# Ordering the first microseconds of a fused attention and GLU kernel: statistics on VectorE, the first tile's K ahead of the second tile's Q, Wk loaded earlier

## The chip, the cores and the metric

The kernel runs on one core of one Trainium2 chip. The metric is the device time of the whole program in microseconds (us), lower is better. Every ratio below is between runs of granted clock 0.999 or 1.0. Times inside a profile count from the start of its span, which is 1.7 to 1.9 us shorter than the measured time.

## The reference, cut to what matters

```python
xn = layernorm(x)                      # x: 1 x 2048 x 512, bf16
a = attention(xn, wqkv, wo)            # 32 heads of 16, a local window of 8 positions, dilation 2
b = (gelu(xn @ w_gate) * (xn @ w_up)) @ w_down
return x + a + b
```

Everything starts with the normalisation of x, and the attention branch starts with Q, K and V = xn @ wqkv. The kernel works on blocks of 512 rows. The first block is cut into four row tiles of 128 rows, so that TensorE can begin before all of it is normalised. For each tile: load x, statistics, subtract the mean, multiply by 1/std (sqrt on ScalarE, reciprocal on VectorE), transpose on TensorE, copy the transpose out of PSUM, project.

## The kernel before

The kernel is a graph of tasks. A list scheduler, when the program is built, orders each engine's tasks from a model of time; `chain([...])` forces an order. The parts that the change touches:

```python
# order of the first loads: a lower prio is issued earlier
x tiles 0, 1, 2, 3:   prio -960, -959, -957.8, -956.5
Wq, Wk, Wv:           prio -958, -957.5, -898

# the second tile (t == 1) has its statistics on ScalarE, in two passes with an accumulator
sx1   = activation(Identity, accum_out=sum)          # sum of x
negm1 = activation(Identity, scale=-1/512)           # minus the mean
sxx1  = activation(Square, bias=-mean, accum_out=..) # sum of squares
...
# warm-up matmuls of ones: WARM[0] ahead of the first transpose, WARM[1] behind it
WARM = ([512] * 9 + [128], [512, 128, 128, 128, 128])
...
# VectorE, ScalarE and TensorE of the first block
chain(["bnst0", "bnag0", "sub0", "rstd0", "norm0", "mean1", "sub1", "evy0_0", "rstd1", "norm1", "evy0_1", "bnst2", ...])
chain(["sx1", "sq0", "negm1", "sxx1", "sq1", "evx0_0", "evx0_1", "evq0_0", "sq2"])
chain(["evx1_0", "sq3"])
chain(WARM[0] + ["tpx0_0"] + WARM[1] +
      ["mma0_0", "tpx0_1", "mmt0_0", "mmt0_1", "mmt1_0", "tpx1_0", "mmt1_1", "mmt0_2", "tpx1_1", ...])
```

In these names `tpx0_0, tpx0_1, tpx1_0, tpx1_1` are the transposes of tiles 0 to 3, and `evx`/`evy` the copies of a transpose by ScalarE and VectorE. `mmt0_t` is Q of tile t (16 matmuls of 128 columns) and `mmt1_t` its K; `mma0_0` is the first half of tile 0's Q, whose other half is then `mmt0_0`. `evq0_t`, `evk0_t` are ScalarE's copies of Q and K out of PSUM, and `sq_t` is a tile's sqrt.

Of the kernel before, what the change touches and what calls it, by code (L numbers as in the profile page):

```python
# [622 lines left out]
BF = mybir.dt.bfloat16  # L623
F32 = mybir.dt.float32
# [47 lines left out]
def bass_parallel_sum__sliding_local_dilated__glu_gated_geglu__prompt_kernel(nc, A_x, A_wqkv, A_wo, B_x, B_w_gate, B_w_up, B_w_down, out, dbg=None, cfg=None):  # L672
# [40 lines left out]
    with contextlib.ExitStack() as es:  # L713
# [29 lines left out]
        sums = sb("sums", [128, 3], F32)  # L743
        XS = sb("XS", [128, 512], BF)
# [64 lines left out]
        I_sums = Item("sums")  # L809
        I_xs = Item("XS")  # L810
        I_junk = Item("junk")
# [54 lines left out]
        for i, wn in enumerate(WARM[0] + WARM[1]):  # L866
            it_warm = Item("warm%d" % i, P_ps, "warm")

            def mk_w(it=it_warm, wn=wn):
                return lambda e: e.matmul(PS[:, 512 * it.slot:512 * it.slot + wn], lhsT=one_l,  # L870
                                          rhs=one_r[:, 0:wn], start=True, stop=True)
            t_w = G.task("pe", "warm%d" % i, d_mm(wn), mk_w(), wr=[it_warm], prio=-400, mode="f")
            t_w.urgent = True
            warm_tasks.append(t_w)
# [43 lines left out]
        for p in range(NP):  # L918
# [5 lines left out]
            if p < 2:  # L924
                for t2 in range(2):
                    def mk_ld(t2=t2, p=p, it=it_x):
                        return lambda e: e.dma_start(  # L927
                            XIN[:, it.slot, t2, :], x2[256 * p + 128 * t2:256 * p + 128 * t2 + 128, :])
                    t_x = G.task("sp", "ld_x%d_%d" % (p, t2), 0, mk_ld(), wr=[(it_x, t2)],
                                 prio=((-960, -959), (-957.8, -956.5))[p][t2], nbytes=128 * 1024)  # L930
            else:
                def mk_ld(p=p, it=it_x):
                    return lambda e: e.dma_start(
                        XIN[:, it.slot, :, :], x2[256 * p:256 * p + 256, :].rearrange("(t q) d -> q t d", q=128))
                t_x = G.task("sp", "ld_x%d" % p, 0, mk_ld(), wr=[(it_x, 0), (it_x, 1)],
                             prio=(0, 0, -897.5, -897)[p] if p < 4 else -950 + p * 20, nbytes=256 * 1024)
# [3 lines left out]
            for t2 in range(2):  # L940
                t = 2 * p + t2

                def mk_st(t=t, t2=t2, it=it_x):
                    return lambda e: e.bn_stats(out=st[:, t, :], in_=XIN[:, it.slot, t2, :])  # L944
                if t == 1:
                    for (nm, dur, kw, rd, wr) in (
                            ("sx1", 0.55, dict(out=XR[:, 0, :], func=ACTF.Identity, accum_out=sums[:, 0:1]),
                             [], [I_junk, (I_sums, 0)]),
                            ("negm1", 0.2, dict(out=sums[:, 1:2], in_=sums[:, 0:1], func=ACTF.Identity,
                                                scale=-1.0 / D), [(I_sums, 0)], [(I_sums, 1)]),  # L950
                            ("sxx1", 0.55, dict(out=XR[:, 0, :], func=ACTF.Square, bias=sums[:, 1:2],
                                                accum_out=sums[:, 2:3]), [(I_sums, 1)], [I_junk, (I_sums, 2)])):
                        def mk_a(kw=kw, it=it_x):
                            return lambda e: e.activation(**dict(dict(in_=XIN[:, it.slot, 1, :]), **kw))
                        t_of[nm] = G.task("act", nm, dur, mk_a(), rd=rd + ([] if "in_" in kw else [(it_x, 1)]),
                                          wr=wr, prio=-300)
                    t_of["mean1"] = G.task("dve", "mean1", 0.1, lambda e: e.tensor_scalar(
                        out=mv[:, 1, 0:1], in0=sums[:, 0:1], scalar1=1.0 / D, scalar2=None, op0=ALU.mult),
                        rd=[(I_sums, 0)], wr=[(I_mv, 1)], prio=tp0(t))
                    continue  # L960
                t_of["bnst%d" % t] = G.task("dve", "bnst%d" % t, 0.6, mk_st(), rd=[(it_x, t2)], wr=[(I_st, t)], prio=tp0(t))

                def mk_ag(t=t):
                    return lambda e: e.bn_aggr(out=mv[:, t, :], in_=st[:, t, :])
                t_of["bnag%d" % t] = G.task("dve", "bnag%d" % t, 0.09, mk_ag(), rd=[(I_st, t)], wr=[(I_mv, t)], prio=tp0(t) + 1)
            for ts in (((2 * p,), (2 * p + 1,)) if b == 0 else ((2 * p, 2 * p + 1),)):
# [6 lines left out]
                def mk_sa(t=t):  # L973
                    if t == 1:
                        return lambda e: e.activation(out=sq[:, 1:2], in_=sums[:, 2:3], func=ACTF.Sqrt,
                                                      scale=1.0 / D, bias=eps[:, 0:1])
                    return lambda e: e.activation(out=sq[:, t:t + 1], in_=mv[:, t, 1:2], func=ACTF.Sqrt,
                                                  bias=eps[:, 0:1])
                if t < NSQA:
                    t_of["sq%d" % t] = G.task("act", "sq%d" % t, 0.15, mk_sa(), rd=[(I_sums, 2) if t == 1 else (I_mv, t), I_eps],  # L980
                                              wr=[(I_sq, t)], prio=pr - 100, table="sqrt")
                else:
                    t_of["ve%d" % t] = G.task("dve", "ve%d" % t, 0.09, mk_ve(), rd=[(I_mv, q) for q in ts],
                                              wr=[(I_ve, q) for q in ts], prio=pr + 1)
# [13 lines left out]
            for t2 in range(2):  # L998
# [6 lines left out]
                if t == 1:  # L1005
                    def mk_sub(it=it_x):
                        return lambda e: e.tensor_scalar(
                            out=XS[:, :], in0=XIN[:, it.slot, 1, :], scalar1=mv[:, 1, 0:1], scalar2=None,
                            op0=ALU.subtract)
                t_of["sub%d" % t] = G.task("dve", "sub%d" % t, 0.27, mk_sub(), rd=[(it_x, t2), (I_mv, t)],  # L1010
                                           wr=[I_xs if t == 1 else (it_x, t2)], prio=tp0(t) + 2)

                def mk_nm(t=t, t2=t2, it=it_x):
                    return lambda e: e.tensor_scalar(  # L1014
                        out=XIN[:, it.slot, t2, :], in0=XS[:, :] if t == 1 else XIN[:, it.slot, t2, :], scalar1=rstd[:, t:t + 1],
                        scalar2=None, op0=ALU.mult)
                t_of["norm%d" % t] = G.task("dve", "norm%d" % t, 0.27, mk_nm(), rd=[I_xs if t == 1 else (it_x, t2), (I_rstd, t)],
# [55 lines left out]
        chain(["bnst0", "bnag0", "sub0", "rstd0", "norm0", "mean1", "sub1", "evy0_0", "rstd1", "norm1",  # L1073
# [5 lines left out]
        for b in range(NB):  # L1079
# [7 lines left out]
            if b == 0:  # L1087
                lead = []
                for t in range(4):
                    for which in range(2):  # L1090
# [17 lines left out]
                        if t == 0 and which == 0:  # L1108
                            t_mm = G.task("pe", "mma0_0", 8 * 0.0563, mk_mm((0, 1)), rd=mrd, wr=[it_mm],
                                          prio=-100, mode="f")  # L1110
                            t_mm.urgent = True
                            t_of["mma0_0"] = t_mm
# [18 lines left out]
                chain(["sx1", "sq0", "negm1", "sxx1", "sq1", "evx0_0", "evx0_1", "evq0_0", "sq2"])  # L1131
                chain(["evx1_0", "sq3"])
                chain(warm_tasks[:len(WARM[0])] + ["tpx0_0"] + warm_tasks[len(WARM[0]):] +
                      ["mma0_0", "tpx0_1", "mmt0_0", "mmt0_1", "mmt1_0", "tpx1_0", "mmt1_1", "mmt0_2", "tpx1_1",
# [428 lines left out]
```

## Time and profile before

| | before |
|---|---|
| median of 3 runs (of all 4) | 194.46 us (194.42) |
| profiled span | 192.5 us |
| TensorE busy | 187.8 us, 98% |
| share of the chain that ended last on TensorE | 95% |
| first transpose, first projection | 4.98, 6.17 us |
| third, fourth transpose | 9.27, 11.28 us |
| end of the first block's Q and K (where the 48 last of these matmuls end in the chain) | 14.35 us |

TensorE is the bound from 14 us to the end (from 14.35 to 180 us it is busy for 164.17 of 165.65 us in this trace), so a time at the end of this first stage is a time at the end of the program. In a timeline line the columns are: start, duration, engine, source line, operation, output and inputs, shape, count, and in brackets how long the engine was idle just before and which work ended that. The lines of before are in the prediction.

### The profile page before, as it was taken

To read this page: it belongs to the slowest core of one execution; us is meant where nothing else is said; L and a number is where in the kernel's file an instruction comes from. 1 tells how busy PE (TensorE), PEld (TensorE's weight loads), DVE (VectorE), ACT (ScalarE), POOL (GpSimd) and SP (SyncE) were. 2 spreads that over 40 slices of the span, in tenths; PEclk is the share of its full clock that TensorE was granted. 3 is DMA by queue.
4 is the path that set the end of the run, shared out by engine and by line. 5 is a ranking of instruction groups with operands and counts; after the bars stand their busy time and mean duration, and the time that the engine had idled before them with its cause. 6 is when DMAs were issued, how large, how long until landed. Compare 5 with 4: busy or idle time off the path is not lost.

```text
span 192.5 us, 3287 instructions
## 1 busy us (share of the span) xinstructions
PE 187.8 (98%) x1244; PEld 92.8 (48%) x1260; DVE 151.7 (79%) x239; ACT 105.9 (55%) x176; POOL 15.6 (8%) x31
## 2 busy tenths in 40 slices
PE   8999999999999999999999999999999999999995
PEld 2894444444444444444444444444444444444484
DVE  5799998999999955999698598998996099912132
ACT  5688574686896766700667587338276720058000
POOL 6010011111931100000000000000000000000000
PEclk9999999999999999999999999999999999999999
DMA  4999998799554033984501497510240496130131
GB/s 141 354 393 329 314 183 167 184 280 207 126 127 109 0 90 85 242 190 110 163 0 50 115 243 170 131 64 0 68 144 9 110 232 160 46 112 0 37 87 44
DMA packets 34800, 27.04 MB, mean 140 GB/s; under 512 B 11264, under 2 KB 33248, under 8 KB 34784
## 3 DMA queue, kind: packets, MB, share of 16 engines
q1 hardware_dynamic: 34784, 26.83, 55.9%
q8 instruction: 10, 0.16, 0.3%
q14 instruction: 6, 0.05, 0.1%
HBM read 19.99 MB, written 5.26 MB: 131 GB/s over the span
## 4 chain that ended last, share of the span: by engine, by line
PE 95%; issue 1%; DMA 1%; DVE 0%; ACT 0%; SPq 0%; DVEq 0%
PE PS L1395 36%; PE PS L1474 20%; PE PS L1152 18%; PE PS L1470 7%; PE PS L1363 4%; PE PS L1098 4%; PE PS L1236 4%; PE PS L1430 2%; DMA XIN<-in_A_x_dram 1%; PE PS L1229 1%; PE PS L1040 1%; PE PS L870 0%; SPq L927 0%; DVE XIN L1014 0%; DVE OB L1494 0%
## 5 line engine op out<-in xcount | busy, mean ns | idle before, releaser
L1474 PE MATMUL PS<-Wd,HT 128*128 128x512 bf16 (+2 forms) x208 | 41.1, 345 | 0.1
L1412 ACT ACTIVATE UU<-PS 128x512 bf16<-128x512 f32 x40 | 24.2, 604 | 29.9 <-PE PS L1395 29.8
L1395 PE MATMUL PS<-xnT,Wu 128*128 128x512 bf16 x155 | 39.7, 379 | 0.6 <-issue 0.5
L1395 PE MATMUL PS<-xnT,Wg 128*128 128x512 bf16 x156 | 39.5, 379 | 0.5 <-issue 0.3
L1206 DVE TENSOR_TENSOR UNI<-QT,KT 128x2048 bf16<-128x2048 bf16 x32 | 37.1, 1218 | 2.6 <-PE PS L1363 2.5
L1152 PE MATMUL PS<-xnT,Wqkv 128*128 128x512 bf16 x157 | 35.2, 379 | 0.2
L1405 ACT ACTIVATE GG<-PS 128x512 bf16<-128x512 f32 x40 | 23.8, 602 | 18.9 <-PE PS L1395 15.9
L1417 DVE TENSOR_TENSOR HT<-GG,UU 128x512 bf16<-128x512 bf16 x40 | 16.4, 416 | 18.1 <-ACT UU L1412 18.0
L1474 PEld LDWEIGHTS PS<-Wd,HT 128*128 128x128 bf16 x209 | 19.6, 98 | 18.5
L1395 PEld LDWEIGHTS PS<-xnT,Wu 128*128 128x128 bf16 x160 | 15.4, 98 | 19.4 <-issue 1.3
L1395 PEld LDWEIGHTS PS<-xnT,Wg 128*128 128x128 bf16 x160 | 15.5, 98 | 19.3 <-issue 0.8
L1152 PEld LDWEIGHTS PS<-xnT,Wqkv 128*128 128x128 bf16 x160 | 15.6, 98 | 18.6
L1343 DVE TENSOR_TENSOR UNI<-BS,PT 128x2048 bf16<-128x2048 bf16 x16 | 19.5, 1221 | 1.9 <-DMA out_dram<-OB 1.8
L1343 DVE TENSOR_TENSOR BS<-BS,PT 128x2048 bf16<-128x2048 bf16 x16 | 19.6, 1224 | 0.4
L1494 DVE TENSOR_TENSOR OB<-PS,XR 128x512 bf16<-128x512 f32 (+2 forms) x19 | 11.4, 604 | 10.5 <-PE PS L1474 10.4
L1470 PE MATMUL PS<-Wo,OT 128*128 128x512 bf16 (+2 forms) x75 | 16.9, 345 | 0.1
L1176 ACT ACTIVATE VT<-PS 128x512 bf16<-128x512 f32 x16 | 9.6, 597 | 4.4 <-PE PS L1152 4.4
L944 DVE BATCH_NORM_STATS2 st<-XIN 128x6 f32<-128x512 bf16 x15 | 10.1, 685 | 1.2 <-DMA XIN<-in_A_x_dram 1.2
L1375 ACT ACTIVATE OT<-PS 128x512 bf16<-128x512 f32 x16 | 8.3, 603 | 5.0 <-PE PS L1363 5.0
L1470 PEld LDWEIGHTS PS<-Wo,OT 128*128 128x128 bf16 x76 | 7.2, 98 | 7.0
L1192 POOL COPY KT<-KT 128x64 bf16<-128x64 bf16 x3 | 7.9, 2639 | 15.2 <-ACT KT L1169 13.8
L1162 ACT ACTIVATE QT<-PS 128x512 bf16<-128x512 f32 x12 | 7.2, 597 | 3.1 <-PE PS L1152 3.1
(74 smaller groups left out, 153.0 us busy)
## 6 DMA issues: line engine op xcount, KB each, us to landing
BS<-vt_scratch SPq DMA_DIRECT2D x64, 128.5 KB, 3.5
vt_scratch<-VT SPq DMA_DIRECT2D x16, 128.0 KB
XR<-in_A_x_dram SPq DMA_DIRECT2D x16, 128.0 KB, 3.4
out_dram<-OB SPq DMA_DIRECT2D x14, 128.0 KB, 1.7
Wqkv<-in_A_wqkv_dram SPq DMA_DIRECT2D x3, 512.0 KB
XIN<-in_A_x_dram SPq DMA_DIRECT2D x6, 256.0 KB, 4.3
Wg<-in_B_w_gate_dram SPq DMA_DIRECT2D x1, 1280.0 KB, 8.1
Wu<-in_B_w_up_dram SPq DMA_DIRECT2D x1, 1280.0 KB
```

What stands on the lines that cost most here:

```text
L944: return lambda e: e.bn_stats(out=st[:, t, :], in_=XIN[:, it.slot, t2, :])
L1152: ins = e.matmul(PS[:, 512 * it.slot:512 * it.slot + HWD], lhsT=lhsT, rhs=xnT[:, itx.slot, kt, c0:c0 + HWD], start=(kt == 0), stop=(kt == 3))
L1176: return lambda e: e.activation(out=VT[:, ito.slot, 0:HWD], in_=PS[:, 512 * it.slot:512 * it.slot + HWD], func=ACTF.Identity)
L1206: return lambda e: e.tensor_tensor(out=UNI[:, it.slot, :, :], in0=bass.AP(QT, (itq.slot * 4 + g) * 512, [[NQT * 4 * 512, 128], [0, 4], [1, ...
L1343: return lambda e: e.tensor_tensor(out=dst(), in0=bass.AP(BS, it.slot * 4 * 514 + o, [[NBS * 4 * 514, 128], [514, 4], [128, 4], [1, 128]]) ...
L1395: ins = e.matmul(PS[0:M, 512 * it.slot:512 * it.slot + 512], lhsT=Wx[:, kt, j * 128:j * 128 + M], rhs=xnT[:, itx.slot, kt, :], start=(kt = ...
L1405: return lambda e: e.activation(out=GG[0:M, ito.slot, :], in_=PS[0:M, 512 * it.slot:512 * it.slot + 512], func=ACTF.Gelu_apprx_tanh)
L1412: return lambda e: e.activation(out=UU[0:M, ito.slot, :], in_=PS[0:M, 512 * it.slot:512 * it.slot + 512], func=ACTF.Identity)
L1417: return lambda e: e.tensor_tensor(out=HT[0:M, ito.slot, j, :], in0=GG[0:M, ig.slot, :], in1=UU[0:M, iu.slot, :], op=ALU.mult)
L1470: ins = e.matmul(PS[:, 512 * it.slot:512 * it.slot + CW], lhsT=OT[:, ito.slot, dq, ti * 128:(ti + 1) * 128], rhs=Wo[:, dq, c0:c1], start=( ...
L1474: ins = e.matmul(PS[:, 512 * it.slot:512 * it.slot + CW], lhsT=HT[:, ith.slot, j, ti * 128:(ti + 1) * 128], rhs=Wd[:, j, c0:c1], start=Fal ...
L1494: return lambda e: e.tensor_tensor(out=OB[:, ito.slot, 0:CW], in0=PS[:, 512 * it.slot:512 * it.slot + CW], in1=XR[:, itx.slot, c0:c1], op= ...
```

## The change

Its intent is to free the first tile's chain of ScalarE's statistics for the second tile, to start TensorE's projections earlier, and to fill a wait behind the second transpose with the first tile's K. Five things are edited: both tiles' statistics go to VectorE; the second set of warm-up matmuls is capped at 128 columns; Wk is issued ahead of the third tile's x; TensorE's order changes; and the second tile's K is split around the third transpose.

```diff
-                                 prio=((-960, -959), (-957.8, -956.5))[p][t2], nbytes=128 * 1024)
+                                 prio=((-960, -959), (-957, -956.5))[p][t2], nbytes=128 * 1024)
...
+                n = min(wn, 128) if i >= len(WARM[0]) else wn
...
-                if t == 1:
-                    for (nm, dur, kw, rd, wr) in (
-                            ("sx1", ...), ("negm1", ...), ("sxx1", ...)):
...                                                    (and all other special cases of t == 1)
-        chain(["bnst0", "bnag0", "sub0", "rstd0", "norm0", "mean1", "sub1", "evy0_0", "rstd1", "norm1",
+        chain(["bnst0", "bnag0", "sub0", "rstd0", "norm0", "bnst1", "evy0_0", "bnag1", "sub1", "rstd1", "norm1",
...
-                        if t == 0 and which == 0:
+                        if t == which:               (mma1_1: half of tile 1's K)
...
-                chain(["sx1", "sq0", "negm1", "sxx1", "sq1", "evx0_0", "evx0_1", "evq0_0", "sq2"])
+                chain(["sq0", "evx0_0", "sq1", "evx0_1", "evq0_0", "sq2"])
...
-                      ["mma0_0", "tpx0_1", "mmt0_0", "mmt0_1", "mmt1_0", "tpx1_0", "mmt1_1", ...
+                      ["mma0_0", "mmt0_0", "tpx0_1", "mmt1_0", "mmt0_1", "mma1_1", "tpx1_0", "mmt1_1", ...
```

More of the change, by code (lines that the diff above doesn't have):

```diff
@@ L742, in bass_parallel_sum__sliding_local_dilated__glu_gated_geglu__prompt_kernel @@
         eps = sb("eps", [128, 1], F32)
-        sums = sb("sums", [128, 3], F32)
-        XS = sb("XS", [128, 512], BF)
         ve = sb("ve", [128, NT], F32)
@@ L808, in bass_parallel_sum__sliding_local_dilated__glu_gated_geglu__prompt_kernel @@
         I_ve = Item("ve")
-        I_sums = Item("sums")
-        I_xs = Item("XS")
-        I_junk = Item("junk")
         I_sq = Item("sq")
@@ L867, in bass_parallel_sum__sliding_local_dilated__glu_gated_geglu__prompt_kernel, with mk_w @@
             it_warm = Item("warm%d" % i, P_ps, "warm")
-            def mk_w(it=it_warm, wn=wn):
-                return lambda e: e.matmul(PS[:, 512 * it.slot:512 * it.slot + wn], lhsT=one_l,
-                                          rhs=one_r[:, 0:wn], start=True, stop=True)
+            def mk_w(i=i, it=it_warm, wn=wn):
+                n = min(wn, 128) if i >= len(WARM[0]) else wn
+                return lambda e: e.matmul(PS[:, 512 * it.slot:512 * it.slot + n], lhsT=one_l,
+                                          rhs=one_r[:, 0:n], start=True, stop=True)
             t_w = G.task("pe", "warm%d" % i, d_mm(wn), mk_w(), wr=[it_warm], prio=-400, mode="f")
@@ L944, in mk_st @@
                     return lambda e: e.bn_stats(out=st[:, t, :], in_=XIN[:, it.slot, t2, :])
-                if t == 1:
-                    for (nm, dur, kw, rd, wr) in (
-                            ("sx1", 0.55, dict(out=XR[:, 0, :], func=ACTF.Identity, accum_out=sums[:, 0:1]),
-                             [], [I_junk, (I_sums, 0)]),
-                            ("negm1", 0.2, dict(out=sums[:, 1:2], in_=sums[:, 0:1], func=ACTF.Identity,
-                                                scale=-1.0 / D), [(I_sums, 0)], [(I_sums, 1)]),
-                            ("sxx1", 0.55, dict(out=XR[:, 0, :], func=ACTF.Square, bias=sums[:, 1:2],
-                                                accum_out=sums[:, 2:3]), [(I_sums, 1)], [I_junk, (I_sums, 2)])):
-                        def mk_a(kw=kw, it=it_x):
-                            return lambda e: e.activation(**dict(dict(in_=XIN[:, it.slot, 1, :]), **kw))
-                        t_of[nm] = G.task("act", nm, dur, mk_a(), rd=rd + ([] if "in_" in kw else [(it_x, 1)]),
-                                          wr=wr, prio=-300)
-                    t_of["mean1"] = G.task("dve", "mean1", 0.1, lambda e: e.tensor_scalar(
-                        out=mv[:, 1, 0:1], in0=sums[:, 0:1], scalar1=1.0 / D, scalar2=None, op0=ALU.mult),
-                        rd=[(I_sums, 0)], wr=[(I_mv, 1)], prio=tp0(t))
-                    continue
                 t_of["bnst%d" % t] = G.task("dve", "bnst%d" % t, 0.6, mk_st(), rd=[(it_x, t2)], wr=[(I_st, t)], prio=tp0(t))
@@ L973, in mk_sa @@
                 def mk_sa(t=t):
-                    if t == 1:
-                        return lambda e: e.activation(out=sq[:, 1:2], in_=sums[:, 2:3], func=ACTF.Sqrt,
-                                                      scale=1.0 / D, bias=eps[:, 0:1])
                     return lambda e: e.activation(out=sq[:, t:t + 1], in_=mv[:, t, 1:2], func=ACTF.Sqrt,
@@ L979, in bass_parallel_sum__sliding_local_dilated__glu_gated_geglu__prompt_kernel @@
                 if t < NSQA:
-                    t_of["sq%d" % t] = G.task("act", "sq%d" % t, 0.15, mk_sa(), rd=[(I_sums, 2) if t == 1 else (I_mv, t), I_eps],
+                    t_of["sq%d" % t] = G.task("act", "sq%d" % t, 0.15, mk_sa(), rd=[(I_mv, t), I_eps],
                                               wr=[(I_sq, t)], prio=pr - 100, table="sqrt")
@@ L1004, in mk_sub @@
                         scalar2=None, op0=ALU.subtract)
-                if t == 1:
-                    def mk_sub(it=it_x):
-                        return lambda e: e.tensor_scalar(
-                            out=XS[:, :], in0=XIN[:, it.slot, 1, :], scalar1=mv[:, 1, 0:1], scalar2=None,
-                            op0=ALU.subtract)
                 t_of["sub%d" % t] = G.task("dve", "sub%d" % t, 0.27, mk_sub(), rd=[(it_x, t2), (I_mv, t)],
-                                           wr=[I_xs if t == 1 else (it_x, t2)], prio=tp0(t) + 2)
+                                           wr=[(it_x, t2)], prio=tp0(t) + 2)
                 def mk_nm(t=t, t2=t2, it=it_x):
                     return lambda e: e.tensor_scalar(
-                        out=XIN[:, it.slot, t2, :], in0=XS[:, :] if t == 1 else XIN[:, it.slot, t2, :], scalar1=rstd[:, t:t + 1],
+                        out=XIN[:, it.slot, t2, :], in0=XIN[:, it.slot, t2, :], scalar1=rstd[:, t:t + 1],
                         scalar2=None, op0=ALU.mult)
-                t_of["norm%d" % t] = G.task("dve", "norm%d" % t, 0.27, mk_nm(), rd=[I_xs if t == 1 else (it_x, t2), (I_rstd, t)],
+                t_of["norm%d" % t] = G.task("dve", "norm%d" % t, 0.27, mk_nm(), rd=[(it_x, t2), (I_rstd, t)],
                                             wr=[(it_x, t2)], prio=tp0(t) + 4)
@@ L1107, in bass_parallel_sum__sliding_local_dilated__glu_gated_geglu__prompt_kernel @@
                         gs = (0, 1, 2, 3)
-                        if t == 0 and which == 0:
-                            t_mm = G.task("pe", "mma0_0", 8 * 0.0563, mk_mm((0, 1)), rd=mrd, wr=[it_mm],
+                        if t == which:
+                            t_mm = G.task("pe", "mma%d_%d" % (which, t), 8 * 0.0563, mk_mm((0, 1)), rd=mrd, wr=[it_mm],
                                           prio=-100, mode="f")
                             t_mm.urgent = True
-                            t_of["mma0_0"] = t_mm
+                            t_of["mma%d_%d" % (which, t)] = t_mm
                             gs = (2, 3)
@@ L1130, in bass_parallel_sum__sliding_local_dilated__glu_gated_geglu__prompt_kernel @@
                                wr=[(it_qt, ("t", t)) if which == 0 else (KTI[0], ("t", t))], prio=-100 + t)
-                chain(["sx1", "sq0", "negm1", "sxx1", "sq1", "evx0_0", "evx0_1", "evq0_0", "sq2"])
+                chain(["sq0", "evx0_0", "sq1", "evx0_1", "evq0_0", "sq2"])
                 chain(["evx1_0", "sq3"])
                 chain(warm_tasks[:len(WARM[0])] + ["tpx0_0"] + warm_tasks[len(WARM[0]):] +
-                      ["mma0_0", "tpx0_1", "mmt0_0", "mmt0_1", "mmt1_0", "tpx1_0", "mmt1_1", "mmt0_2", "tpx1_1",
+                      ["mma0_0", "mmt0_0", "tpx0_1", "mmt1_0", "mmt0_1", "mma1_1", "tpx1_0", "mmt1_1", "mmt0_2", "tpx1_1",
                        "mmt1_2", "mmt0_3", "mmt1_3"])
```

## The prediction

> **What bounds the kernel now.** I read the page's busy shares and its chain first, to see which engine sets the end; then the timelines of the four engines over the first 15 us, because every edit lies there; then the waits of the DMA queue, because one edit moves a load.
>
> ```profile
> PE 187.8 (98%) x1244; PEld 92.8 (48%) x1260; DVE 151.7 (79%) x239; ACT 105.9 (55%) x176; POOL 15.6 (8%) x31
> ...
> PE 95%; issue 1%; DMA 1%; DVE 0%; ACT 0%; SPq 0%; DVEq 0%
> ```
>
> TensorE is busy for 98% of a span of 192.5 us (194.46 us measured, so some 2 us are outside the span), and 95% of the chain that ended last is its work. From a table of stages: from 14.35 to 180 us it is busy 164.17 of 165.65 us. So nothing later can repay much, and a microsecond saved at the start should reach the end nearly whole, if the later order stays. At the start 0.8 us pass before any matmul and about 5.3 us go to warm-up matmuls of ones and to waiting for the first row tile; real projections begin at 6.17. TensorE in order of time:
>
> ```profile
> 4.98 0.61 PE L1040 MATMUL PS<-ident,XIN 128*128 128x128 bf16 x4
> 5.38 0.95 PE L870 MATMUL PS<-const-bfloat16-1.0 128*128 128x512 bf16 x5
> 6.17 0.61 PE L1098 MATMUL PS<-xnT,Wqkv 128*128 128x128 bf16 x8
> 6.61 0.39 PE L1040 MATMUL PS<-ident,XIN 128*128 128x128 bf16 x4
> 6.83 2.60 PE L1098 MATMUL PS<-xnT,Wqkv 128*128 128x128 bf16 x40
> 9.27 0.39 PE L1040 MATMUL PS<-ident,XIN 128*128 128x128 bf16 x4
> 9.49 1.95 PE L1098 MATMUL PS<-xnT,Wqkv 128*128 128x128 bf16 x32
> 11.28 0.39 PE L1040 MATMUL PS<-ident,XIN 128*128 128x128 bf16 x4
> 11.51 2.84 PE L1098 MATMUL PS<-xnT,Wqkv 128*128 128x128 bf16 x48
> ```
>
> Each group of four is the transpose of one row tile; between the groups are the Q and K projections of 128 rows. The starts give the rates: 32 matmuls lie between 9.49 and 11.28, 1.79 us, so **0.056 us each**, a half (8) is 0.45, a tile's Q or K (16) 0.90, a transpose group 0.22. The whole stage is 128 matmuls and three transposes, 7.17 + 0.66 = 7.83 us; its first matmul counts from about 6.33 in the chain and its end is 14.35, 8.02, so it holds only about **0.2 us of waits**. The waits name that one: the weight load at L1098 waited 0.2 us for ScalarE's copy of the second tile's transpose (7.04 to 7.42).
>
> [...] warm-up matmuls of 512 columns start 0.43 us apart until about 6.0 and 128-column matmuls follow at 0.056 us later. [...] the load issued behind a wait for Wk starts only at 7.66.
>
> **The change, part by part.**
>
> (1) Statistics of the second tile leave ScalarE. The accumulated sum (0.63 plus its read 0.19), the scaled mean (0.19), the square pass (0.72 plus 0.19) go; VectorE loses a 0.15 us mean and gains a 0.69 us statistics pass and a 0.18 us aggregate. For the first tile:
>
> ```profile
> 3.43 0.63 ACT L954 ACTIVATE XR<-XIN 128x512 bf16<-128x512 bf16 x1 [1.14 <-DMA XIN<-in_A_x_dram]
> 3.96 0.19 ACT L954 ACTIVATION_READ_ACCUMULATOR XR<-XIN 128x1 f32 x1
> 4.06 0.28 ACT L977 ACTIVATE sq<-mv,eps 128x1 bf16<-128x1 bf16 x1
> ```
>
> VectorE's aggregate for the first tile ends at 3.87, yet the sqrt starts at 4.06; for the third tile the same pair is 8.14 and 8.18. So the first sqrt is free to start at about 3.91, end by 4.21, and the reciprocal (now 4.37) then waits for the 0.35 to 0.40 us subtraction to get out of the way, to about 4.26. **Gain about 0.11 us**: transpose at 4.87.
>
> (2) Warm-up. Of the five matmuls between the first transpose and the first projection, one shrinks from 512 to 128 columns: 0.32 us less[...]. Now they end at about 6.17, while the copy of the first transpose ends at 6.01. A copy's end to the next matmul is 0.05 to 0.06 us (7.42 to 7.47), so the projection would start at 6.07 on that alone, and with (1) at 5.96. **Gain of (1) and (2) together: 0.2 us.** About 0.14 us idle opens before it, less than the queueing saved.
>
> (3) The first tile's whole Q precedes the second transpose: 5.96 + 0.90 = 6.86. The second tile on VectorE: statistics at about 4.73 to 5.42, copy of the first transpose 5.51, aggregate 5.71, then, by the third tile's distance from aggregate to normalisation (7.96 to 8.71, 0.75), normalisation 6.46 to 6.81, transpose possible at 6.87. It just meets the PE. Then the first tile's K (0.90) covers the copy of this transpose, so **the old 0.2 us wait goes**. It needs Wk at 7.09.
>
> (4) Wk is queued ahead of the third tile's x. Before, Wk landed at about 7.62:
>
> ```profile
> SPq L888 <- DMA Wqkv<-in_A_wqkv_dram: 1.5, 1, 1.5
> 7.66 0.37 SPq L888 DMA_DIRECT2D Wg<-in_B_w_gate_dram  x1
> ```
>
> The 128 KB of x no longer ahead, at some 380 GB/s of that stretch, are 0.35 us: Wk lands at about 7.28, so the K matmuls wait **0.1 to 0.25 us**. The third x takes Wk's old place, up to 7.6; its statistics are wanted at 7.51 (0.20 after the copy of the second transpose, 7.31) and it becomes transposable about 1.87 later (7.24 to 9.11 before), so at 9.4 to 9.5. TensorE gets there at 7.08 + 40 x 0.056 = 9.32 without, about 9.5 with the Wk wait. These two waits overlap and are not added.
>
> (5) The second tile's K is split, 8 before the third transpose and 8 after. This **opens a new wait**. The copy of the third transpose:
>
> ```profile
> 9.70 0.60 ACT L1060 ACTIVATE xnT<-PS 128x512 bf16<-128x512 bf16 x1 [0.52 <-PE PS L1040]
> 10.19 0.29 ACT L977 ACTIVATE sq<-mv,eps 128x1 bf16<-128x1 bf16 x1
> ```
>
> It starts 0.43 after the transpose, takes 0.60, and a matmul follows 0.06 later: 1.09 us. Before, 0.22 + 16 x 0.056 = 1.12 covered it exactly. Now 0.22 + 0.45 = 0.67 covers it, and the next task, the third tile's Q, needs that copy: **0.42 us of waiting**. The fourth tile's normalisation comes 1.84 after the third transpose (11.06 less 9.22) and TensorE needs it after 1.99, so no second wait.
>
> The sum at the fourth transpose: third transpose at 9.32 to 9.57, midpoint 9.45, plus 0.22 + 0.45 + 0.42 + 0.90 = 11.44, against 11.28 before. So +0.16 us, from 0.03 to 0.28. In another form: 0.2 earlier start and 0.2 wait removed, against 0.42 at the third tile and 0.1 to 0.2 for Wk or normalisation. Everything after is shifted: 194.46 + 0.16 = **194.6 us**.
>
> **The rivals.** (A) The new waits are smaller than I think: x and Wk land early, and the copy's wait is partly covered. For: my landing times are from a mean rate. Against: the copy's 1.09 us is measured. Then the 0.4 us gain stands less some 0.2: 194.2. (B) The compile-time list scheduler orders every later instruction from its own model of time, with priorities tuned for the old start; other starts can flip choices, and the late TensorE order with them. For: it is one greedy pass. Against: less than 1.5 us is idle from 14.35 to 180 now, and DVE and ACT have slack. It could add 0 to 0.7 us: up to 195.3.[...]
>
> **Range and chances.** The start alone gives 194.3 to 194.8 with the landing times uncertain; (B) pushes mainly upward, so 194.1 to 195.2 holds eight in ten. Two per cent is 3.9 us; none of the effects[...] reaches it, so within 2% gets 0.98, and 0.01 each is left for the unforeseen.
>
> **What would show it.** Right: first sqrt near 3.91, first transpose near 4.87, first projection near 5.96, no wait at the second tile's copy; a wait of about 0.42 us at L1098 for ScalarE's third copy; Wg's issue near 7.3; the third transpose at 9.3 to 9.6 and the fourth at 11.3 to 11.6. Wrong: a first projection still near 6.17, Wk landed before 7.1, no wait behind the third transpose,[...] or TensorE idle between 14 and 180 us that differs from 1.5 us by more than 0.3.

Two figures of the text are my estimates. The 0.32 us of warm-up is three quarters of the 0.43 us between the starts of 512-column warm-up matmuls; 128-column ones start 0.10 to 0.11 us apart in the trace before (5.81, 5.91) and in the one after (5.25, 5.36, 5.46, 5.57). The 0.35 us of Wk is 128 KB at the 380 GB/s that I took (the trace before shows 362 from 4.0 to 7.6 us), and assumes that the bytes ahead of a load set its landing.

## The result, and the profile after

The changed kernel takes **195.24 us** (median of 4 runs, 194.84 to 195.26) against 194.42 us. The ratio is 1.0042 with a 95% interval of 1.0026 to 1.0058. The ratios are not always the ratio of the medians quoted. The result is within 2%, as forecast, but 0.04 us above the stated range, and five times the predicted rise (0.82 instead of 0.16 us).

The page of the changed kernel, its busy shares and its chain that ended last:

```profile
PE 189.5 (98%) x1260; PEld 92.7 (48%) x1260; DVE 152.5 (79%) x240; ACT 104.3 (54%) x171; POOL 10.2 (5%) x31
...
PE 94%; DMA 3%; ACT 1%; SPq 1%; DVE 0%; issue 0%; DVEq 0%
```

Nothing has changed in kind: TensorE bounds the kernel. But 3% of the chain, 5.5 us, is now a load, where before it was 1%. (The 1.5 us of later TensorE idle that the prediction counted can be put down to missing records: the trace before holds 1244 matmul records and this one 1260, and from 14.35 to 180 us it has 995 matmuls to 1010 weight loads. In this trace TensorE is busy for all of that stretch, 165.65 us. So the prediction's sign about this idle time says nothing.)

TensorE of the changed kernel in the first stage, to be held against the nine rows of before in the prediction:

```profile
4.85 0.61 PE L1012 MATMUL PS<-ident,XIN 128*128 128x128 bf16 x4
5.25 0.74 PE L866 MATMUL PS<-const-bfloat16-1.0 128*128 128x128 bf16 x5
6.37 1.05 PE L1070 MATMUL PS<-xnT,Wqkv 128*128 128x128 bf16 x16 [0.38 <-DVE XIN L979]
7.26 0.39 PE L1012 MATMUL PS<-ident,XIN 128*128 128x128 bf16 x4
7.77 2.41 PE L1070 MATMUL PS<-xnT,Wqkv 128*128 128x128 bf16 x40
10.30 0.40 PE L1012 MATMUL PS<-ident,XIN 128*128 128x128 bf16 x4
10.53 0.61 PE L1070 MATMUL PS<-xnT,Wqkv 128*128 128x128 bf16 x8
11.38 1.07 PE L1070 MATMUL PS<-xnT,Wqkv 128*128 128x128 bf16 x16 [0.24 <-ACT xnT L1032]
12.29 0.39 PE L1012 MATMUL PS<-ident,XIN 128*128 128x128 bf16 x4
```

The first transpose and the warm-up behind it are 0.13 us earlier than before. From there on everything is later: the first projection by 0.20 us, the third transpose by 1.03 us, the fourth by 1.01 us, the end of the stage (15.35) by 1.00 us; the span is 1.0 us longer. So all of the loss is made before the third transpose. The chain of waits from there, in order of time (start, duration, what):

```profile
2.19 5.53 DMA Wqkv<-in_A_wqkv_dram
...
7.77 1.08 PE PS L1070 x16
...
8.88 0.60 ACT KT L1097
9.47 0.19 ACT sq L954
...
10.30 0.41 PE PS L1012 x4
```

The lines left out after the sqrt are the reciprocal and the normalisation on VectorE, and short steps marked as issue. This is one chain: Wk lands at 7.72, only then can the first tile's K be computed, ScalarE copies it out, and *behind that copy in ScalarE's queue* stands the third tile's sqrt, whose input had been ready at 9.03. The third transpose inherits the landing of Wk through a sqrt that has nothing to do with Wk.

The third tile's x is late too, since it is now loaded behind Wk (that order alone moved its statistics from 7.24 to 7.74, b_wk_first below). VectorE of the changed kernel:

```profile
7.69 0.29 DVE L1024 COPY xnT<-PS 128x256 bf16<-128x256 bf16 x1 [0.90 <-PE PS L1012]
8.12 0.69 DVE L940 BATCH_NORM_STATS2 st<-XIN 128x6 f32<-128x512 bf16 x1
```

The statistics start 0.43 us after the start of the copy ahead of them in the queue, where before it was 0.20 us (7.04 and 7.24): the load of this x, issued at 2.74, took 5.4 us to land. Without the wait for the sqrt, x would have let the third transpose start at about 9.99 (8.12 plus the prediction's 1.87), and TensorE's own work ahead of it, held by Wk, ends at 10.01 (7.77 + 40 x 0.056). So these two waits overlap, and the sqrt adds the rest, up to 10.30.

### The profile page after: what moved, and what is told of

Its sections match the earlier page's. It is cut to its first block, busy times and chain, and to the rows that moved or that the text cites. A ratio compares the mean times of both kernels' runs of the same rounds, so it can differ in the third digit from the quotient of the medians.

```text
span 193.5 us, 3299 instructions
## 1 busy us (share of the span) xinstructions
PE 189.5 (98%) x1260; PEld 92.7 (48%) x1260; DVE 152.5 (79%) x240; ACT 104.3 (54%) x171; POOL 10.2 (5%) x31
## 4 chain that ended last, share of the span: by engine, by line
PE 94%; DMA 3%; ACT 1%; SPq 1%; DVE 0%; issue 0%; DVEq 0%
PE PS L1367 36%; PE PS L1446 20%; PE PS L1124 18%; PE PS L1442 7%; PE PS L1335 4%; PE PS L1208 4%; DMA Wqkv<-in_A_wqkv_dram 3%; PE PS L1070 2%; PE PS L1402 2%; PE PS L1201 1%; SPq L923 0%; PE PS L1012 0%; ACT xnT L1032 0%; ACT KT L1097 0%; SPq L875 0%
## 5 line engine op out<-in xcount | busy, mean ns | idle before, releaser
L1367 PE MATMUL PS<-xnT,Wu 128*128 128x512 bf16 x160 | 40.9, 379 | 0.0
L1367 PE MATMUL PS<-xnT,Wg 128*128 128x512 bf16 x160 | 40.3, 379 | 0.0
L1124 PE MATMUL PS<-xnT,Wqkv 128*128 128x512 bf16 x160 | 35.7, 379 | 0.0
L940 DVE BATCH_NORM_STATS2 st<-XIN 128x6 f32<-128x512 bf16 x16 | 10.9, 686 | 1.4 <-DMA XIN<-in_A_x_dram 1.2
L1141 ACT ACTIVATE KT<-PS 128x512 bf16<-128x512 f32 x12 | 7.2, 598 | 2.9 <-PE PS L1124 2.9
```

Of the source, the lines that this page charges most:

```text
L940: return lambda e: e.bn_stats(out=st[:, t, :], in_=XIN[:, it.slot, t2, :])
L1124: ins = e.matmul(PS[:, 512 * it.slot:512 * it.slot + HWD], lhsT=lhsT, rhs=xnT[:, itx.slot, kt, c0:c0 + HWD], start=(kt == 0), stop=(kt == 3))
L1367: ins = e.matmul(PS[0:M, 512 * it.slot:512 * it.slot + 512], lhsT=Wx[:, kt, j * 128:j * 128 + M], rhs=xnT[:, itx.slot, kt, :], start=(kt = ...
```

## The experiments

Each kernel was timed in five rounds against the kernel before on the same chip. All twelve gave a correct result. The stage end is the end of the first block's Q and K in the chain of each trace. One of b_best's six executions was slow (196.94 us at a clock of 0.991): its ratio leaves it out, its median does not (194.25 us without it).

| run | stage end | span less stage end | median | ratio to before, 95% interval |
|---|---|---|---|---|
| before | 14.35 | 178.2 | 194.34 to 194.48 | 1 |
| change | 15.35 | 178.2 | 195.24 | 1.0042 (1.0026 to 1.0058) |
| after_again | 15.04 | 178.2 | 195.07 | 1.0035 (1.0016 to 1.0053) |
| b_dve_stats | 14.40 | 178.2 | 194.33 | 0.9999 (0.9982 to 1.0016) |
| b_warm_cut | 14.28 | 178.2 | 194.26 | 0.9991 (0.9975 to 1.0008) |
| b_wk_first | 14.71 | 178.2 | 194.75 | 1.0026 (1.0009 to 1.0043) |
| b_pe_order | 15.25 | 178.2 | 195.41 | 1.0049 (1.0032 to 1.0065) |
| b_pe_order_sq2 | 14.96 | 178.2 | 194.85 | 1.0033 (1.0009 to 1.0058) |
| a_sq2_first | 15.10 | 178.2 | 194.84 | 1.0022 (1.0006 to 1.0037) |
| a_no_split | 15.62 | 178.2 | 195.19 | 1.0044 (1.0028 to 1.0061) |
| a_old_load_order | 15.46 | 178.2 | 195.45 | 1.0059 (1.0043 to 1.0075) |
| a_act_queue | 15.49 | 178.2 | 195.45 | 1.0064 (1.0037 to 1.0091) |
| b_best | 14.06 | 178.2 | 194.31 | 0.9988 (0.9968 to 1.0008) |
| b_best_again | 14.16 | 178.2 | 194.14 | 0.9981 (0.9965 to 0.9997) |

The third column decides rival (B) of the prediction. The list scheduler did choose another later order in the changed kernel: the instruction lists of all engines but GpSimd differ beyond the first stage. Yet from the end of the stage to the end of the span it takes 178.2 us in every one of the fourteen traces (178.19 to 178.21 with the spans as the traces keep them, unrounded). Later reordering shows no effect; the whole difference lies in the first 15 us.

### The change once more

> The changed kernel as it is, on the same chip as the runs beside it, and a second trace of it. Both theories: 195.1 to 195.3 us, and 0.8 us over before. The landing of Wq (first projection 6.37 in the first trace) and of Wk (first K matmul 7.77) should be within 0.3 us of these; that is how far I take one trace's landing times to scatter, since two kernels with the same first 8 us differed by 0.27 us at the first projection.

No edit. Median 195.07 us, just under what I expected, and 0.6 us over before instead of 0.8. In this trace the first projection starts at 6.05, the first K matmul at 7.46, the third transpose at 9.99. These are 0.32, 0.31 and 0.31 us earlier than in the first trace, a little more than the scatter that I had allowed, and everything behind moved with them. So one trace's landing times scatter by 0.3 us. The 0.29 us between the end of TensorE's work ahead of the third transpose (7.46 + 40 x 0.056 = 9.70) and the transpose itself is the same in both traces.

### The parts, one at a time, on the kernel before

**Statistics on VectorE and the free first sqrt alone** (the changed kernel with load order, warm-up, split and TensorE order put back):

```diff
-                      ["mma0_0", "mmt0_0", "tpx0_1", "mmt1_0", "mmt0_1", "mma1_1", "tpx1_0", ...
+                      ["mma0_0", "tpx0_1", "mmt0_0", "mmt0_1", "mmt1_0", "tpx1_0", ...
   (and (-957.8, -956.5), the 512-column warm-up, and no mma1_1)
```

> The change's statistics on VectorE and the freed first sqrt alone, with the warm-up, load order and TensorE order of before. Theory: first transpose at 4.87 instead of 4.98, second tile normalised at about 6.8 instead of 6.37, so that the second transpose waits from about 6.55 to 6.85 behind the first 8 projections; third transpose at 9.4 to 9.6; time up by 0.1 to 0.3 us. Rival (the undisturbed first chain is a gain by itself): time down by 0.1 us or more.

The first transpose comes at 4.87, as expected; the third at 9.33, the stage ends at 14.40, and the ratio is 0.9999. The 0.1 us won at the first tile is used up by the later second tile. By itself this part is worth nothing either way; neither theory's size was right. (No edit of mine explains one thing in this trace: with the same ten warm-up matmuls ahead of it, the last three of them, from 3.77, took 0.69 us instead of the 1.17 of the trace before, and then the four matmuls of the first transpose 0.40 us instead of 0.61. What sets this was not shown.)

**The shorter warm-up alone:**

```diff
+                n = min(wn, 128) if i >= len(WARM[0]) else wn
```

> The kernel before with the shortened warm-up alone (one matmul of 512 columns becomes 128). Prediction on record (the warm-up held the first projection): first projection near 6.07 instead of 6.17. Rival (Wq's landing holds it just behind the warm-up): first projection stays between 6.1 and 6.4, with an idle gap ahead of it of 0.3 us or more, and the time does not fall: within 0.15 us of before or up to 0.2 us over it.

The first projection starts at 6.09, where the prediction said 6.07. The stage ends 0.07 us earlier. The time does not separate from before (0.9975 to 1.0008), and the rival's late landing is not seen with this load order.

**The load order alone:**

```diff
-  (-957.8, -956.5)
+  (-957, -956.5)
```

> The kernel before with the load order of the change alone. Theory 1 (Wk behind Wq delays Wq): first projection at 6.3 to 6.4 instead of 6.17, time up by about 0.2 us; Wk is not needed before 8.37, so its landing costs nothing. Theory 2 (Wq's landing does not depend on the order): first projection at 6.17 and the time within 0.1 us of before. Theory 3 (bytes ahead set Wk's landing): Wg's issue, which waits for Wk, moves from 7.66 to about 7.3.

The first projection stays at 6.11, which is Theory 2's, and the issue of Wg (the gate weights), which waits for Wk, comes at 7.34, which is Theory 3's and my own 7.28; as the five traces below show, that was the earliest landing of this order and no proof of the sum. But the time rises by 0.4 us, which no theory had. VectorE and TensorE in this trace:

```profile
7.74 0.69 DVE L944 BATCH_NORM_STATS2 st<-XIN 128x6 f32<-128x512 bf16 x1 [0.45 <-DMA XIN<-in_A_x_dram]
...
9.63 0.40 PE L1040 MATMUL PS<-ident,XIN 128*128 128x128 bf16 x4 [0.23 <-DVE XIN L1014]
```

The third tile's x now lands at about 7.70, its statistics start 0.50 us later than before (7.24), and the third transpose waits. In the kernel before, Wk is not needed until about 8.4, so bringing it forward buys nothing and the x behind it pays.

**TensorE's order alone**, without the split:

```diff
-                      ["mma0_0", "tpx0_1", "mmt0_0", "mmt0_1", "mmt1_0", "tpx1_0", ...
+                      ["mma0_0", "mmt0_0", "tpx0_1", "mmt1_0", "mmt0_1", "tpx1_0", ...
```

> The kernel before with TensorE's order of the change alone, without the split: first tile's Q whole, second transpose, first tile's K, second tile's Q. Theory (K is asked for before Wk has landed): the first K matmul is ready at about 7.29 and waits for Wk until 7.6 to 7.9, the third transpose comes at 9.5 to 9.8 instead of 9.27, and the time grows by 0.2 to 0.5 us. Rival (the order is good, and the statistics on VectorE or the load order spoil it): no wait for Wk over 0.1 us, the old 0.2 us wait gone, time down by 0.1 to 0.2 us.

This one edit costs 195.41 us, ratio 1.0049, as much as the whole change and about twice the most that I expected. TensorE, then ScalarE, in this trace:

```profile
7.63 1.96 PE L1098 MATMUL PS<-xnT,Wqkv 128*128 128x128 bf16 x32 [0.39 <-DMA Wqkv<-in_A_wqkv_dram]
10.16 0.40 PE L1040 MATMUL PS<-ident,XIN 128*128 128x128 bf16 x4 [0.57 <-DVE XIN L1014]
...
8.74 0.60 ACT L1125 ACTIVATE KT<-PS 128x512 bf16<-128x512 f32 x1 [0.58 <-PE PS L1098]
9.23 0.29 ACT L977 ACTIVATE sq<-mv,eps 128x1 bf16<-128x1 bf16 x1
```

There are two waits. The K matmuls wait for Wk, and then the third transpose waits 0.57 us for its normalisation. Its aggregate on VectorE was done at 8.39, but the sqrt ran only at 9.23: ScalarE sat idle for 0.58 us, with the copy of K at the head of its queue, waiting for matmuls that waited for Wk.

### Is it ScalarE's queue?

The copy of K is put behind the third tile's sqrt, first in the kernel with TensorE's order alone, then in the changed kernel. The edit is the same:

```diff
-  chain([..., "evx0_1", "evq0_0", "sq2"])
+  chain([..., "evx0_1", "evq0_0", "sq2", "evk0_0"])
```

> The kernel before with TensorE's new order alone (which cost 0.95 us) and ScalarE's copy of the first tile's K put behind the third tile's sqrt. Theory (half of that loss is the sqrt queued behind a copy that itself waits for Wk): third tile's sqrt at about 8.45 instead of 9.23, third transpose at about 9.45 to 9.7 instead of 10.16 with no wait for its normalisation, time down by 0.4 to 0.6 us from 195.41; what stays, 0.3 to 0.5 us over before, is the wait for Wk. Rival (the wait for Wk alone holds the stage): third transpose still after 10.0 and the time within 0.1 us of 195.4.

TensorE and ScalarE of the first:

```profile
9.65 0.39 PE L1040 MATMUL PS<-ident,XIN 128*128 128x128 bf16 x4
...
8.57 0.30 ACT L977 ACTIVATE sq<-mv,eps 128x1 bf16<-128x1 bf16 x1 [0.27 <-DVE mv L964]
```

The sqrt now waits for VectorE and not for a copy, and the third transpose has no idle ahead of it although Wk landed later here (K matmuls at 7.85). From the first K matmul to the third transpose it takes 1.80 us here and 2.53 us in b_pe_order. The median falls by 0.56 us, from 195.41 to 194.85, as the theory asked, though two of the six runs were at 195.5 and 195.8 and the intervals of the ratios overlap; the stage end of the two traces falls by 0.29 us. What stays over before is the wait for Wk, and a new one that the theory had not: the copy of the third transpose now stands behind a copy of Q on ScalarE, and TensorE waits 0.23 us for it (10.99).

> The changed kernel with ScalarE's copy of the first tile's K put behind the third tile's sqrt. In the changed kernel that copy (8.88, 0.60 us) stands ahead of the sqrt (9.37 instead of about 9.07). Theory 1 (the queue order on ScalarE costs the third transpose 0.3 us): third transpose near 10.0 instead of 10.30, no wait ahead of it, time down by 0.25 to 0.3 us. Rival (the third transpose is held by the late x of the third tile, whose statistics began at 8.12): third transpose stays at 10.2 to 10.3 and the time within 0.1 us of the changed kernel.

ScalarE of the changed kernel, then ScalarE and TensorE of this run:

```profile
8.88 0.60 ACT L1097 ACTIVATE KT<-PS 128x512 bf16<-128x512 f32 x1 [0.32 <-PE PS L1070]
9.37 0.29 ACT L954 ACTIVATE sq<-mv,eps 128x1 bf16<-128x1 bf16 x1
...
9.11 0.30 ACT L954 ACTIVATE sq<-mv,eps 128x1 bf16<-128x1 bf16 x1 [0.44 <-DVE mv L944]
...
7.81 2.41 PE L1070 MATMUL PS<-xnT,Wqkv 128*128 128x128 bf16 x40
10.05 0.39 PE L1012 MATMUL PS<-ident,XIN 128*128 128x128 bf16 x4
```

In the changed kernel the sqrt moves from 9.37 to 9.11, the third transpose from 10.30 to 10.05, and its wait is gone (7.81 + 2.24 = 10.05). The median is 194.84, 0.2 to 0.4 us below the two timings of the change; the intervals of the ratios overlap, so it is the trace that carries this verdict. The stage end, 15.10, does not settle it either: it lies between those of the change's two traces (15.35 and 15.04), whose landings differ. But one comparison is free of the landings' scatter. In all six traces in which the copy of K stands ahead of the sqrt and K ahead of the third transpose, the third transpose starts 2.53 us after the first K matmul; here it is 2.24 us, which is TensorE's own work. The third tile's x does not hold it longer either: its normalisation ends at 9.98.

### Is it the split?

```diff
-  if t == which:                                   "mmt0_1", "mma1_1", "tpx1_0", "mmt1_1"
+  if t == 0 and which == 0:                        "mmt0_1", "tpx1_0", "mmt1_1"
```

> The changed kernel without the split of the second tile's K: all 16 matmuls behind the third transpose, as before. Theory 1 (the third transpose waits for its normalisation, so that the split only moved the wait): the 0.42 us wait for the third copy goes, the wait ahead of the third transpose grows from 0.3 to about 0.75 us, third transpose still at 10.3, and the time within 0.1 us of the changed kernel. Rival (the split itself costs the 0.42 us that I predicted): time down by 0.4 us.

```profile
6.67 1.05 PE L1070 MATMUL PS<-xnT,Wqkv 128*128 128x128 bf16 x16 [0.86 <-DMA Wqkv<-in_A_wqkv_dram]
...
10.54 0.40 PE L1012 MATMUL PS<-ident,XIN 128*128 128x128 bf16 x4 [0.57 <-DVE XIN L986]
```

The 0.42 us wait behind the third transpose is gone, and the wait ahead of it has grown from 0.29 to 0.74 us (8.01 + 32 x 0.056 = 9.80). The third transpose again starts 2.53 us after the first K matmul. The time, 195.19 us, is that of the change. The split moves a wait; it is neither the cause nor a gain. The first of these lines shows something else. In the changed kernel the gap ahead of the first projection was put down to VectorE's subtraction for the second tile, which this projection does not read; its two copies had ended by 5.87. Here, with the same instructions up to that point, the trace names the load of Wq, and the projection starts 0.3 us later still. So in the changed kernel the wait for Wq is inferred, not named by its own trace.

### Is it the load order within the changed kernel?

```diff
-  (-957, -956.5)
+  (-957.8, -956.5)
```

> The changed kernel with one thing put back: the third tile's x is again issued ahead of Wk. In the changed kernel the first projection began at 6.37 although its operand was copied by 5.87; I read this as a wait for Wq. Theory 1 (Wk's load directly behind Wq makes Wq land later): the first projection begins at or before 6.15 here, Wk still lands near 7.7, so the first K matmuls still begin near 7.75 and the time stays within 0.1 us of the changed kernel. Theory 2 (Wq lands near 6.3 in either order and the kernel before hid it under its longer warm-up): the first projection stays at 6.3 to 6.4. Theory 3 (the bytes ahead of Wk set its landing, as I predicted): Wk lands some 0.35 us later than in the changed kernel, near 8.05, and the time grows by 0.3 us.

The first projection starts at 6.07 and Wk lands at about 7.82, both as Theory 1 says, and Theory 3's 8.05 is not seen. The time, 195.45 us, is 0.2 to 0.4 us over the change instead of equal to it. Of the five traces with Wk directly behind Wq on SyncE, the first projection came at 6.37, 6.05, 6.11, 6.40 and 6.67; in the seven traces of altered kernels with x between them, at 5.96 to 6.11. That speaks for a later Wq with the new order, but 6.11 and 6.05 are among the five, so I do not call it shown. What is shown is that the bytes ahead of a load do not fix its landing as closely as I reckoned: Wg's issue, which follows Wk's landing, was at 7.34, 7.43, 7.74, 7.78 and 7.98 with the new order, and at 7.60 to 7.84 with the old. With the new order the landings move together: in the four traces of the changed kernel and its variants with this order Wg's issue follows the first projection by 1.31 to 1.38 us, and in all five the third tile's statistics follow Wg's issue by 0.36 to 0.40 us. The mean rate does not explain the spread: from 0.5 to 6.6 us four of the five, b_wk_first, the change's first trace, a_sq2_first and a_no_split, moved 219, 212, 208 and 215 GB/s, with the first projection at 6.11, 6.37, 6.40 and 6.67.

### Can the landings be brought forward?

The change, with Wq and Wk issued from ScalarE at once:

```diff
+            t_w.on_act = nm in "qk"
```

> The changed kernel with the loads of Wq and Wk issued from ScalarE at its very start, where it is idle, instead of third and fourth from SyncE. Theory (two weight landings cost the changed kernel about 0.4 us at the first projection and 0.28 us at the first K matmul): both waits shrink to under 0.1 us unless the first x tiles land later for it; first projection near 6.0, first K matmul near 7.1, time down by 0.3 to 0.7 us. Rival (the landings are not what holds them): time within 0.1 us of the changed kernel. If the x tile lands later instead, the first transpose moves from 4.85 to 5.1 or later, and the gain is that much smaller.

A miss, though its last sentence allowed for a late x: the first transpose comes at 5.15. VectorE and TensorE:

```profile
5.67 0.69 DVE L941 BATCH_NORM_STATS2 st<-XIN 128x6 f32<-128x512 bf16 x1 [0.57 <-DMA XIN<-in_A_x_dram]
6.28 0.27 DVE L1025 COPY xnT<-PS 128x256 bf16<-128x256 bf16 x1
...
6.66 1.05 PE L1071 MATMUL PS<-xnT,Wqkv 128*128 128x128 bf16 x16 [0.81 <-ACT xnT L1033]
```

The weights are now issued from 0.80 on, at the same time as the x tiles. The second tile's statistics start at 5.67 instead of 4.71, 0.96 us later, because its x lands late; what held that load was not shown, but this edit is the only one. Behind them in VectorE's queue stands its half of the copy of the *first* transpose, 6.28 to 6.55, and so the first projection starts at 6.66. ScalarE's half had ended by 5.97; the bracket names only one of the two copies. It is the same mistake as the sqrt behind the copy, on another engine, and it hides whether Wq was there sooner. The time is 195.45 us, 0.2 to 0.4 us over the change.

### A version that follows from this

Two things of the kernel before were left to gain, 0.1 us of warm-up and the 0.2 us wait for the second tile's copy. The second goes without asking for K early: cut the first tile's Q 4 and 12 instead of 8 and 8, so that the second transpose comes sooner and more matmuls cover its copy.

```diff
+                n = min(wn, 128) if i >= len(WARM[0]) else wn
...
-                            t_mm = G.task("pe", "mma0_0", 8 * 0.0563, mk_mm((0, 1)), ...
+                            t_mm = G.task("pe", "mma0_0", 8 * 0.0563, mk_mm((0,)), ...
...
-                        t_mm = G.task("pe", "mmt%d_%d" % (which, t), 4 * len(gs) * 0.0563, mk_mm(gs), ...
+                        t_mm = G.task("pe", "mmt%d_%d" % (which, t), 4 * len(gs) * 0.0563, mk_mm((1, 2, 3) if t == which == 0 else gs), ...
```

> The kernel before with the shortened warm-up and the first tile's Q cut 4 and 12 instead of 8 and 8 around the second transpose. Theory (what is left to gain is the 0.2 us wait for the second copy and 0.1 us of warm-up): second transpose near 6.42, held by its normalisation, no wait for its copy, third transpose near 9.1; time 0.1 to 0.3 us under before, so 194.1 to 194.3. Rival (Wq's landing or the next normalisation takes it back): time within 0.05 us of before.

Median 194.31 (194.25 without the slow execution), interval 0.9968 to 1.0008, third transpose at 8.99; open, so it was run again.

> The same kernel as b_best (before, shortened warm-up, first Q cut 4 and 12) once more, because its interval of 0.9968 to 1.0008 left open whether it beats the kernel before. If the trace's gain at the third transpose (8.99 instead of 9.27) is real and carries through, the ratio lies at 0.998 to 0.999 again, 0.2 to 0.4 us under before; if it was chance, at 1.000 or over.

```profile
6.63 2.62 PE L1099 MATMUL PS<-xnT,Wqkv 128*128 128x128 bf16 x44
9.09 0.39 PE L1041 MATMUL PS<-ident,XIN 128*128 128x128 bf16 x4
```

The 44 matmuls run from 6.63 to the third transpose at 9.09, 2.46 us, which is 44 x 0.056: no wait for the second copy is left. Median 194.14 us, ratio 0.9981 (0.9965 to 0.9997). It beats before by 0.3 to 0.4 us in this timing, while the first left it open; by the stage end it gains 0.29 and 0.19 us. Against the change, b_best's 194.25 us stands beside 195.07 us on the same chip. That is small, well inside 2%, but it comes from the same two sources in both traces.

## Why the prediction was right or wrong

| step | predicted | first trace | second trace |
|---|---|---|---|
| first sqrt | 3.91 | 3.90 | 3.87 |
| first transpose | 4.87 | 4.85 | 4.85 |
| second tile's normalisation starts | 6.46 | 6.44 | 6.44 |
| first projection | 5.96 | 6.37 | 6.05 |
| first K matmul | 7.09, plus 0.1 to 0.25 | 7.77 | 7.46 |
| third tile's statistics | 7.51, its x landed by 7.6 | 8.12 | 7.79 |
| third transpose | 9.32 to 9.57 | 10.30 | 9.99 |
| third to fourth transpose | 1.99 | 1.99 | 1.99 |

- **Steps (1) and (3), right.** The chain of the first two tiles came within 0.04 us at each point, and the old wait for the second copy is gone (40 matmuls without a gap from 7.77).
- **Step (2), mechanism right, size cut off.** On the kernel before, the shorter warm-up gave 6.09 for 6.07. In the change the operand was copied by 5.87, but the projection started at 6.37, by all signs for want of Wq. The prediction had no term for Wq: the kernel before, whose warm-up lasted until 6.17, showed no wait for it, and I took its landing to be early.
- **Step (4), the term that was mis-sized.** "Wk lands at about 7.28": in the first trace it landed at 7.72, and the five traces with this order spread over 0.64 us. The K matmuls started 0.29 and 0.23 us later than the second transpose allowed (7.26 + 0.22 = 7.48 and 7.01 + 0.22 = 7.23), after a late start already. That these waits come near the predicted 0.1 to 0.25 us is luck: in the first trace TensorE asked for Wk at 7.48 instead of 7.09, and Wk was later by about as much. The third tile's x was late as well (8.12 and 7.79 instead of 7.51). A mean rate times the bytes ahead did not give the landing time here (7.28 reckoned; 7.72 in the first trace). (The rate itself is not to blame: the trace before gives 362 GB/s from 4.0 to 7.6 us where I wrote 380, which is 0.01 us.)
- **Step (4), the sentence that failed.** "These two waits overlap and are not added." For the landings of Wk and of x that held (10.01 and 9.99 in the first trace). But I held the normalisation of the third tile to its load alone. It also stands behind ScalarE's copy of the first tile's K, and so behind Wk: the waits are in series. That adds 0.29 us in both traces of the change. Putting the sqrt ahead of the copy removed it, and took 0.56 us off the median of the kernel with TensorE's order alone.
- **Step (5), right and without weight.** The new wait behind the third transpose was 0.42 us as worked out, and 1.99 us to the fourth transpose held exactly. But taking the split back changed nothing, because the third transpose then waits instead. Counting it as a loss was right only on the assumption that TensorE, not the normalisation, set the third transpose.
- **The sum.** The upper end predicted for the third transpose, 9.57, plus 0.44 us of later Wk and 0.29 us of queued sqrt is the 10.30 of the first trace; in the second, 0.14 and 0.29 us give 10.00 for 9.99. The measured median is 0.64 us over the predicted 194.6.
- **The rivals.** (A) is out. (B), the scheduler's later order, did occur and cost nothing: 178.2 us in both. A slower TensorE is hardly seen: the first 16 projections take 0.89 us (6.37 to 7.26) in the first trace, the 0.056 us each of the trace before, and 0.96 us (6.05 to 7.01), 0.060 each, in the second.
- **Range and chances.** Within 2% was right. The upper bound missed by 0.04 us, since I let only rival (B) push upward and gave the landings too small a spread.

What stays open is what makes a weight's landing scatter by 0.6 us between traces of the same order, and whether Wk directly behind Wq delays Wq. No run tried the changed kernel with the first tile's K back behind the second tile's Q and all else kept.

## What to carry to other kernels

Before asking for an operand earlier, find out when it is there, in a kernel that really waits for it; a trace without a wait only gives an upper bound, and one trace does not give the scatter (0.3 us between the two traces of the change). When an instruction will now wait for something new, look at what stands behind it on its engine: in b_pe_order a 0.29 us sqrt ran behind a copy, 0.84 us after its input was ready (8.39 and 9.23), and so passed the wait for Wk on to a tile that did not need Wk. And if the time to the end from one point of the trace is constant over all variants, as 178.2 us was here, read every variant at that point, where the scatter of the whole run does not hide a tenth of a microsecond.
